# Attention and two expert layers on one core: the value product on 64x64 tiles, with whole in-weight loads

## The chip, the cores and the metric

The kernel runs on one core of a Trainium2 chip. The core has a matrix engine (TensorE; PE is its matmuls, PEld its loads of weights), a vector engine (DVE), a scalar engine (ACT), GpSimd (POOL) and a sync engine (SP), which here issues every DMA. The metric is device time in microseconds. Three runs of the kernel before gave 1185.9, 1187.23 and 1188.79 us; the median is 1187.23 us.

## The reference

```python
def _attn_ref(q, k, v, mem_k, mem_v):          # (4, 8, 768, 64); memory: 8 tokens a head
    chunk, left_ctx, right_ctx = (32, 16, 8)
    for c in range(nc):
        ...
        k_full = np.concatenate([mem_k, k_ctx], axis=2)
        v_full = np.concatenate([mem_v, v_ctx], axis=2)
        scores = scale * np.matmul(q_c, k_full.transpose(0, 1, 3, 2))
        scores = scores - np.max(scores, axis=-1, keepdims=True)
        a = np.exp(scores)
        a = a / (np.sum(a, axis=-1, keepdims=True) + 1e-09)
        out[:, :, c_start:c_end] = np.matmul(a, v_full)

def _moe_ref(x, w_in, w_out):                  # 3072 tokens, 512 -> 2048 -> 512
    h = x @ w_in
    g = h * (1.0 / (1.0 + np.exp(-1.702 * h)))
    return (g @ w_out).astype(np.float32)

def _moe2_ref(x, w_gate, w_val, w_out):        # 512 -> 1536 -> 512
    g = x @ w_gate
    silu = g * (1.0 / (1.0 + np.exp(-g)))
    val = x @ w_val
    return (silu * val @ w_out).astype(np.float32)
```

Attention runs in chunks of 32 queries, each over 64 keys (8 memory tokens, 16 to the left, 32, 8 to the right). Its output, with the heads side by side as 512 features, goes through the two feed-forward layers.

## The kernel before

The 3072 tokens are 24 groups of 128 tokens (four chunks of 32) and six blocks of four groups. For each group the kernel computes the scores of 8 heads, the exponents and their sums on DVE and ACT, and weights divided by the sums. The matrix engine turns the weights (`turn`, L153), so that the keys lie along the partitions: partition 64e + k holds key k of head 2a + e, with a from 0 to 3. `keep_e` copies them from PSUM to `ebd` (L162). The value product (`values`, L169) takes from there. `keep_x` and, in the first block, `hi_x` and `lo_x` copy the result to where the first layer reads it, and `store_x` writes it to memory.

Before the change `ebd` is block diagonal: for a pair a and a chunk c it holds 64 columns, 32 for each head e, and zeros in the other head's 64 rows, which two memsets (`zero`, L674) write once. A matmul of the value product therefore has all 128 rows, the 64 features of two heads' values as stationary columns (`v[:, a + j, c, :]`) and 64 moving columns. The result of pair a + j goes to partitions 64j and up, so that features stand in the order (pair within two, head). To match, the first layer's in-weights are loaded with their rows in that order: `load_raw` splits each of these tiles into two DMAs with a rearranged source (L276), for the 16 pairs of tiles that hold in-weights. All other weight tiles come in one DMA (L271).

The work of the opening is written out as a list of short names (`OPENING`), which sets the order of every engine: `ldq`, `ldk`, `ldv`, `ldw` are loads (queries, keys, values, weights), `sc` scores, `te` the turn, `ec` the copies of `keep_e`, `pv` the value product, `ua` and `ub` the first products with the in-weights (L542), `z` memsets. In the opening the scores of the first eight groups use 64-row tiles (L706), with the two heads' scores in two PSUM banks; later groups use a block-diagonal key tile and 128 rows (L196). After the opening the attention of blocks 2 to 5 is laid between the products of the first layer (L446 up, L581 down) at fixed places of a unit. SP's order after the opening is left to the scheduler.

Of the kernel before, what the change touches and what calls it, by code (L numbers as in the profile page):

```python
# [10 lines left out]
F32 = mybir.dt.float32  # L11
# [8 lines left out]
P = 128  # L20
B, H, S, D = 4, 8, 768, 64
NM = 8
CH, LEFT, RIGHT = 32, 16, 8
# [7 lines left out]
HP = H // 2  # L31
KC = DM // P
NF1, NF2 = FF1 // P, FF2 // P
BLK = 512
NBLK = NT // BLK
GRP = BLK // P
# [21 lines left out]
def tile_attention_moe_moe(  # L58
# [8 lines left out]
    nc = tc.nc  # L67
# [24 lines left out]
    def bank(name):  # L92
        return psum["p"].tile([P, BLK], F32, tag="p", name=name)
# [3 lines left out]
    apool = attn_ctx.enter_context(tc.tile_pool(name="attn", bufs=1))  # L97
    kbd = apool.tile([P, 2, HP, 4, KW], F32, name="kbd")
    vm = [apool.tile([P, HP, 4, D], F32, name=f"vm{i}") for i in range(2)]
    ebd = [apool.tile([P, HP, 4, 2, CH], F32, name="ebd")]  # L100

    qt, et, rt, xq, xf = {}, {}, {}, {}, {}

    def off_diagonal(t, eng):
        eng.memset(t[0:64, 1], 0.0)
        eng.memset(t[64:128, 0], 0.0)
# [43 lines left out]
    def turn(ps, t):  # L150
        ps = ps.rearrange("p (a q) -> p a q", a=HP)
        for a in range(HP):
            nc.tensor.transpose(ps[:, a, :], t[:, 2 * a : 2 * a + 2, :], ident)  # L153
        return ps

    def weights_at(g):
        return ebd[g % 2 if g < 2 * GRP else 0]

    def keep_e(g, ps, engs):
        for e, copy in enumerate(engs):  # L160
            r = slice(64 * e, 64 * e + 64)
            copy(weights_at(g)[r, :, :, e, :], ps[r].rearrange("p a (c q) -> p a c q", c=4))  # L162

    def values(g, ps, v):
        ps = ps.rearrange("p (a q) -> p a q", a=KC)
        for a in range(0, HP, 2):
            for c in range(4):
                for j in range(2):
                    nc.tensor.matmul(  # L169
                        ps[64 * j : 64 * j + 64, a : a + 2, CH * c : CH * c + CH],  # L170
                        v[:, a + j, c, :],
                        weights_at(g)[:, a + j, c].rearrange("p e q -> p (e q)"),
                        start=True,
                        stop=True,
                    )
        return ps

    def keep_x(g, ps):
# [27 lines left out]
        st_exp(g)  # L206

    def st_et(g):
        keep_e(g, turn(bank("ps_t"), et.pop(g)), (nc.scalar.copy,) * 2)

    def st_pv(g):
        ps = values(g, bank("ps_o"), vm[g % 2])
        if g + 2 < NG:
            load_kv("v", g + 2)
        keep_x(g, ps)
        store_x(g)
# [42 lines left out]
    raws = []  # L259
    AT = (0, 1, 4, 5, 2, 3, 6, 7)  # L260

    def load_raw(upto):
        while len(raws) < min(upto, NRAW):
            i = len(raws)
            if RB <= i < RB + len(spare_raw):
                raws.append(spare_raw[i - RB])
            else:
                raws.append(rpool.tile([P, 512], I64, tag="raw", name="raw", bufs=RB))
            k = AT[i] if i < len(AT) else i
            if k >= 2 * NF1 or k % 4 > 1:  # L270
                nc.sync.dma_start(out=raws[-1], in_=wr[k])  # L271
                continue
            src = wr[k].rearrange("(e d) (b a n) -> a d b e n", e=2, b=2, a=2)
            for a in range(2):
                dst = raws[-1][64 * a : 64 * a + 64].rearrange("d (b e n) -> d b e n", b=2, e=2)
                nc.sync.dma_start(out=dst, in_=src[a])  # L276

    nraw, bits = [2 * len(AT)], {}

# [21 lines left out]
    def next_weights(out):  # L301

        i = nraw[0]
        load_raw(i + RB)
        nraw[0] += 1
        take_words(i)
        yield 0
        shift_words(i)
        yield 0
        join_words(i)  # L310
        out += [bits.pop(i), raws[i]]
# [338 lines left out]
    spare = [wt["spare", i].rearrange("p s n -> p (s n)") for i in range(SPARE)]  # L650
# [1 line left out]
    k_open = [kbd[:, g] for g in range(2)]  # L652
    k_open += [spare[6 + i].bitcast(F32).rearrange("p (a c k) -> p a c k", a=HP, c=4) for i in range(6)]
    v_open = vm + [spare[12].bitcast(F32).rearrange("p (a c d) -> p a c d", a=HP, c=4)]
    ebd.append(spare[13].bitcast(F32).rearrange("p (a c e q) -> p a c e q", a=HP, c=4, e=2))
    for i in range(SPARE):
        give_w(("spare", i))
    xh, xl = [[bpool.tile([P, 2, BLK], F32R, tag="b", name=n) for _ in range(2)] for n in ("xh", "xl")]
    V, G = nc.vector, nc.gpsimd
    firsts, pairs, at, tok = [[None] * 2 for _ in range(PLAIN)], [], {}, []  # L660
# [7 lines left out]
            qt[g] = pairs[-1][:, g % 2].bitcast(F32).rearrange("p (a q) -> p a q", a=HP)  # L668
        nc.sync.dma_start(out=qt[g], in_=qg[g])

    def zero(n):
        if n < 2:
            for e in range(2):
                (V, G)[n].memset(ebd[n][64 * e : 64 * e + 64, :, :, 1 - e, :], 0.0)  # L674
        else:
            off_diagonal(kbd, G)

    def table():
        t = apool.tile([P, H], F32, tag="m", name="t", bufs=2)
# [69 lines left out]
    def values_first(g):  # L749
        at["x", g] = values(g, bank("ps_v"), vm[g % 2] if g >= 2 * GRP else v_open[g % 3])  # L750
# [118 lines left out]
    def tokens():  # L869
# [3 lines left out]

    DO = {
        "z": zero,
        "tb": lambda _: table(),
        "ldq": load_q,
        "ldk": lambda g: load_kv_first("k", g),
        "ldv": lambda g: load_kv_first("v", g),
        "ldw": lambda i: load_raw(i + 1),  # L880
        "st": store_x,
        "sc": scores_first,
# [4 lines left out]
        "rc": st_reciprocal,  # L887
        "wg": weigh_first,
        "te": turned,
        "ec": lambda g: keep_e(g, at.pop(("e", g)), (nc.scalar.copy,) * 2),  # L890
        "pv": values_first,
        "hi": hi_x,
        "xf": keep_first,
# [55 lines left out]
        "ts": lambda k, *e: tokens().sum(k, *e),  # L949
    }  # L950
    OPENING = """
        z0 tb0 z1 ldq0 ldk0 ldw0 ldq1 ldk1 ldk2 ldk3 ldq2 sc0 ldq3 mx0 pr0 ldw1 cs0 ex0 ldq4 ct0 sc1 ldv0 sm0
        wa0 wal0 ra0 ldv1 mx1 z2 ldq5 sc2 ldk4 rc0 ex1 wg0 ldk5 sm1 te0 mx2 ra1 sc3 ec0 ldw2 rc1 wg1 ex2 ldk6
        pr1 sm2 ldk7 te1 cs1 ra2 rc2 ct1 ldq6 pv0 ec1 wg2 ldq7 sumA0 mx3 wb0 ldv2 wv0 te2 hi0 wvl0 sc4 ex3 ldv3
        wbl0 xl0 ec2 sumB0 sm3 sc5 mx4 ra3 xf0 pv1 ldw3 hiB0 rc3 ex4 loB0 wg3 ldv4 pr2 mx5 te3 hi1 ldw4 ec3 cs2
# [47 lines left out]
    def attention(b):  # L1003
        gs = range(GRP * b, GRP * b + GRP)
        steps = [[(st_scores, gs[0])]]
        for g in gs:
            steps.append([(st_et, g)] + ([(st_scores, g + 1)] if g < gs[-1] else []))
            steps.append([(st_pv, g)])
        return steps
# [25 lines left out]
    for n, (ph, b, ua, ub) in enumerate(seq):  # L1035
# [6 lines left out]
        for u in range(ua, ub):  # L1042
# [47 lines left out]
            if u == ua and nxt is not None and not attends:  # L1090
                src = {1: xd, 2: yd}[nxt[0]][nxt[1]]
# [55 lines left out]
```

## Time and profile before

| | PE busy | DVE | ACT | POOL |
|---|---|---|---|---|
| whole span, 1184.9 us | 1151.1 (97%) | 653.3 (55%) | 568.2 (48%) | 342.4 (29%) |
| 0 to 19.3 us | 7.09 | 9.46 | 6.29 | 4.80 |
| 19.3 to 40.4 us | 13.62 | 16.19 | 14.17 | 7.48 |
| 140 to 278 us | 137.34 | 82.63 | 70.99 | 21.16 |

The profiled execution's span, from its first to its last instruction, is 1184.9 us; the runs' times are 1185.9 us and up, and what lies between is outside the span. Times of the table are busy us in each stretch. A busy engine is one with an instruction in flight; matmuls overlap one another, so 97% does not say that the array is full. A matmul in f32 leaves two records in the trace, each with its load of weights.

### The profile page before, as it was taken

Reading aid. Unit: us, or ns where it says so; the run is one execution under the profiler, and the core shown is the slowest. Engines: PE = TensorE matmul, PEld = TensorE weight load, DVE = VectorE, ACT = ScalarE, POOL = GpSimd, SP = SyncE. Lnnn points to the kernel's source line nnn. Section 1 sums busy time; section 2 is a strip of 40 time slices with the busy share of each in tenths; the row PEclk is TensorE's granted clock in tenths of the full one; section 3 lists DMA queues with packets and bytes.
Section 4 is the critical chain, followed back from the end, with each engine's and each line's share of the span. In section 5 each row is a group of like instructions: output and inputs, shape, how many; then the busy total and the mean of one; then the engine's idle time right before and its main releaser. Section 6 shows DMA issues by size and latency. Waiting matters only on the chain.

```text
span 1184.9 us, 22299 instructions
## 1 busy us (share of the span) xinstructions
PE 1151.1 (97%) x8908; PEld 1038.1 (88%) x8908; DVE 653.3 (55%) x1129; ACT 568.2 (48%) x1185; POOL 342.4 (29%) x309
## 2 busy tenths in 40 slices
PE   4899999999999999999999999999999999999998
PEld 3778788888899999999998989999999999999997
DVE  6786756565765444443456555354565554454553
ACT  5776554545565454444455544343445533243342
POOL 3354230203544242321235433021345521021110
PEclk9899999999999999999999999999999999999999
DMA  9986644351452322421333321210225130320302
GB/s 319 286 260 188 169 134 140 111 160 60 137 170 98 117 80 90 142 69 57 107 119 113 108 90 36 72 71 1 90 90 177 36 106 2 108 98 11 108 25 83
DMA packets 62920, 131.47 MB, mean 111 GB/s; under 512 B 5728, under 2 KB 26208, under 8 KB 60512
## 3 DMA queue, kind: packets, MB, share of 16 engines
q1 hardware_dynamic: 62816, 130.05, 35.0%
q8 instruction: 70, 1.15, 0.4%
q14 instruction: 34, 0.28, 0.1%
HBM read 98.57 MB, written 31.46 MB: 110 GB/s over the span
## 4 chain that ended last, share of the span: by engine, by line
PE 87%; DMA 4%; DVE 4%; ACT 2%; issue 2%; SPq 0%; POOL 0%; DVEq 0%; ACTq 0%; POOLq 0%
PE y L581 36%; PE ps_a L446 27%; PE ps_c L446 12%; PE ps_b L446 8%; PE ps_s L196 1%; PE ps_o L169 1%; DMA vm<-in_vg 1%; DMA w<-in_kg 1%; PE ps_u L542 1%; DMA qq<-in_qg 1%; DMA xd<-xf 1%; PE ps_t L153 1%; DMA raw<-in_wr 1%; PE ps_v L169 1%; DVE b L432 0%
## 5 line engine op out<-in xcount | busy, mean ns | idle before, releaser
L446 PEld LDWEIGHTS ps_a<-b,w 128*128 128x128 f32 x2832 | 384.0, 189 | 40.1 <-DVE ps_a L498 6.1
L446 PE MATMUL ps_a<-b,w 128*128 128x256 f32 x2832 | 397.6, 283 | 5.5 <-DVE ps_a L498 3.5
L581 PE MATMUL y<-gs,w 128*128 128x512 f32 x1152 | 298.2, 394 | 0.9 <-DVE e L742 0.5
L581 PE MATMUL y<-w,gs 128*128 128x512 f32 x864 | 247.9, 395 | 0.6 <-DVE gs L561 0.4
L581 PEld LDWEIGHTS y<-gs,w 128*128 128x128 f32 x1152 | 204.2, 189 | 36.8 <-DVE gs L561 1.2
L446 PE MATMUL ps_c<-b,w 128*128 128x256 f32 x1224 | 179.1, 282 | 0.0
L446 PEld LDWEIGHTS ps_c<-b,w 128*128 128x128 f32 x1224 | 167.1, 190 | 8.8
L581 PEld LDWEIGHTS y<-w,gs 128*128 128x128 f32 x864 | 144.1, 190 | 14.7 <-DVE gs L561 2.1
L253 POOL TENSOR_TENSOR w<-wf,w 128x512 fp32r<-128x512 f32 (+1 forms) x66 | 76.3, 1158 | 232.2 <-ACT w L250 214.8
L446 PE MATMUL ps_b<-b,w 128*128 128x256 f32 x900 | 133.7, 285 | 1.1 <-ACT m L847 0.8
L446 PEld LDWEIGHTS ps_b<-b,w 128*128 128x128 f32 x900 | 118.9, 191 | 4.6 <-issue 1.5
L549 ACT ACTIVATE g<-ps_b 128x512 f32<-128x512 f32 x72 | 43.1, 598 | 166.6 <-DVE ps_b L504 166.6
L432 DVE TENSOR_TENSOR b<-xl,b 128x512 fp32r<-128x512 f32 x72 | 64.7, 898 | 80.4 <-ACT b L428 80.2
L498 DVE TENSOR_TENSOR ps_a<-m,ps_a 128x256 f32<-128x256 f32 x115 | 49.0, 426 | 105.4 <-PE ps_a L446 99.3
L488 ACT COPY u<-ps_a 128x256 f32<-128x256 f32 x115 | 43.0, 374 | 106.6 <-PE ps_a L446 106.4
L411 POOL TENSOR_TENSOR xl<-xl,t 128x512 f32<-128x512 f32 x18 | 23.3, 1295 | 231.2 <-DVE t L408 229.9
L561 DVE TENSOR_TENSOR gs<-ps_a,gs 128x512 fp32r<-128x512 f32 x118 | 80.9, 685 | 10.2 <-ACT gs L557 9.9
L483 DVE TENSOR_TENSOR ps_b<-p,ps_b 128x256 f32<-128x256 f32 x115 | 49.2, 428 | 61.0 <-PE ps_b L446 54.8
L557 ACT CAST gs<-ps_a 128x512 fp32r<-128x512 f32 x118 | 69.8, 592 | 23.0 <-DVE ps_a L527 15.8
L527 DVE TENSOR_TENSOR ps_a<-g,ps_a 128x512 f32<-128x512 f32 x72 | 50.0, 694 | 45.7 <-PE ps_a L446 45.2
L479 ACT COPY p<-ps_a 128x256 f32<-128x256 f32 x115 | 43.0, 374 | 59.9 <-PE ps_a L446 55.9
L504 DVE TENSOR_TENSOR ps_b<-u,ps_c 128x256 f32<-128x256 f32 x102 | 43.5, 427 | 50.1 <-PE ps_c L446 49.8
(131 smaller groups left out, 1181.4 us busy)
## 6 DMA issues: line engine op xcount, KB each, us to landing
raw<-in_wr SPq DMA_DIRECT2D x49, 512.0 KB, 3.4
xl<-yd SPq DMA_DIRECT2D x12, 1024.0 KB, 4.8
vm<-in_vg SPq DMA_DIRECT2D x22, 512.0 KB, 4.6
kbd<-in_kg SPq DMA_DIRECT2D x32, 256.0 KB, 4.2
raw<-in_wr SPq DMA_DIRECT2D x30, 256.0 KB, 5.0
yp<-o SPq DMA_DIRECT2D x24, 256.0 KB, 2.7
xl<-xd SPq DMA_DIRECT2D x6, 1024.0 KB, 4.8
base<-yp SPq DMA_DIRECT2D x24, 256.0 KB, 3.4
```

The source lines that it names most:

```text
L253: eng.tensor_sub(w[:, 1, o : o + n], f, w[:, 0, o : o + n].bitcast(F32))
L432: (eng or self.engs[k]).tensor_sub(x[:, 1], self.source(k), x[:, 0].bitcast(F32))
L446: nc.tensor.matmul(ps, w[:, a, o + kc * P : o + kc * P + P], x[:, c, kc, :], start=(start and kc == 0 and (a, c) == PASSES[0]), stop=(kc = ...
L479: nc.scalar.copy(p1, ca[:, :n])
L483: add(cb[:, :n], p1, cb[:, :n])
L498: add(ca[:, n:], m, ca[:, :n])
L504: add(cb[:, n:], u2, cc)
L527: late[0] = [lambda: nc.vector.tensor_mul(ca, t, ca), lambda: gs.append(cast(ca))]
L549: nc.scalar.activation(t, c, AF.Silu)
L557: nc.scalar.copy(x[:, 0], g)
L561: nc.vector.tensor_sub(x[:, 1], g, x[:, 0].bitcast(F32))
L581: nc.tensor.matmul(y, lhs, rhs, start=(first and o == 0 and (a, c) == PASSES[0]), stop=(ends and o == len(gs) - 1 and (a, c) == passes[-1]),)
```

## The change

The value product is computed head by head: 64 rows (the keys of one head), 64 stationary columns (its features) and 32 moving columns (the queries of one chunk), into partitions 64e and up. `ebd` and its zeros go; the turned weights are copied once, as they stand, into `ek`, which has two buffers. The features then stand in their natural order, and the in-weight tiles are loaded whole, in one DMA each.

```diff
-    ebd = [apool.tile([P, HP, 4, 2, CH], F32, name="ebd")]
+    ek = [apool.tile([P, HP, P], F32, name=f"ek{i}") for i in range(2)]
...
-    def keep_e(g, ps, engs):
-        for e, copy in enumerate(engs):
-            r = slice(64 * e, 64 * e + 64)
-            copy(weights_at(g)[r, :, :, e, :], ps[r].rearrange("p a (c q) -> p a c q", c=4))
+    def keep_e(g, ps):
+        nc.scalar.copy(ek[g % 2], ps)
 
     def values(g, ps, v):
         ps = ps.rearrange("p (a q) -> p a q", a=KC)
-        for a in range(0, HP, 2):
+        for a in range(HP):
             for c in range(4):
-                for j in range(2):
-                    nc.tensor.matmul(
-                        ps[64 * j : 64 * j + 64, a : a + 2, CH * c : CH * c + CH],
-                        v[:, a + j, c, :],
-                        weights_at(g)[:, a + j, c].rearrange("p e q -> p (e q)"),
-                        start=True,
-                        stop=True,
-                    )
+                q = slice(CH * c, CH * c + CH)
+                for e in range(2):
+                    h = slice(64 * e, 64 * e + 64)
+                    nc.tensor.matmul(ps[h, a, q], v[h, a, c, :], ek[g % 2][h, a, q], start=True, stop=True)
...
-            k = AT[i] if i < len(AT) else i
-            if k >= 2 * NF1 or k % 4 > 1:
-                nc.sync.dma_start(out=raws[-1], in_=wr[k])
-                continue
-            src = wr[k].rearrange("(e d) (b a n) -> a d b e n", e=2, b=2, a=2)
-            for a in range(2):
-                dst = raws[-1][64 * a : 64 * a + 64].rearrange("d (b e n) -> d b e n", b=2, e=2)
-                nc.sync.dma_start(out=dst, in_=src[a])
+            nc.sync.dma_start(out=raws[-1], in_=wr[AT[i] if i < len(AT) else i])
...
-    def zero(n):
-        if n < 2:
-            for e in range(2):
-                (V, G)[n].memset(ebd[n][64 * e : 64 * e + 64, :, :, 1 - e, :], 0.0)
-        else:
-            off_diagonal(kbd, G)
+    def zero(_):
+        off_diagonal(kbd, G)
...
-        z0 tb0 z1 ldq0 ldk0 ldw0 ldq1 ldk1 ldk2 ldk3 ldq2 sc0 ldq3 mx0 pr0 ldw1 cs0 ex0 ldq4 ct0 sc1 ldv0 sm0
+        tb0 ldq0 ldk0 ldw0 ldq1 ldk1 ldk2 ldk3 ldq2 sc0 ldq3 mx0 pr0 ldw1 cs0 ex0 ldq4 ct0 sc1 ldv0 sm0
```

The order of PE around the third and fourth value bursts of the opening, before (`ps_v` is the result, `ps_t` the turned weights, `ps_k` scores, `ps_u` the first products with the in-weights):

```order
L706 MATMUL ps_k_128<-w,qq 32x64 x32
L169 MATMUL ps_v<-ebd,w 64x2x32 x16
L169 MATMUL ps_v<-w,vm_117 64x2x32 x16
L706 MATMUL ps_k_128<-w,qq 32x64 x32
L153 MATMUL ps_t<-ident,e 128x128 x4
L542 MATMUL ps_u<-xh,w 128x512 x8
```

Each of the two bursts is 16 matmuls of 64 moving columns (2x32). The same place of PE's order after the change:

```order
L685 MATMUL ps_k_129<-w,qq 32x64 x32
L166 MATMUL ps_v<-ek_119,w 64x32 x32
L166 MATMUL ps_v<-ek_120,vm_117 64x32 x32
L685 MATMUL ps_k_129<-w,qq 32x64 x32
L153 MATMUL ps_t<-ident,e 128x128 x4
L526 MATMUL ps_u<-xh,w 128x512 x8
```

Nothing else stands in another place on PE: each value burst has 32 matmuls with 32 moving columns in place of 16 with 64.

The start of SP's order of issues, before (`q`, `qq` queries, `kbd` and `w` from `in_kg` keys, `raw` and `w` from `in_wr` weights, `vm` and `w` from `in_vg` values):

```order
L276 DMA raw<-in_wr 64x4x128 x2
L669 DMA q<-in_qg 128x512
L689 DMA vm_117<-in_vg 128x1024
L689 DMA vm_118<-in_vg 128x1024
L669 DMA q<-in_qg 128x512
L687 DMA w<-in_kg 128x1024 x2
L276 DMA raw<-in_wr 64x4x128 x2
L687 DMA w<-in_kg 128x1024 x2
L669 DMA qq<-in_qg 128x512 x2
L689 DMA w<-in_vg 128x1024
L689 DMA vm_117<-in_vg 128x1024
L276 DMA w<-in_wr 64x4x128 x2
```

Each in-weight tile is two issues here (x2). The same place of SP's order after the change:

```order
L260 DMA raw<-in_wr 128x512
L652 DMA q<-in_qg 128x512
L668 DMA vm_117<-in_vg 128x1024
L668 DMA vm_118<-in_vg 128x1024
L652 DMA q<-in_qg 128x512
L666 DMA w<-in_kg 128x1024 x2
L260 DMA raw<-in_wr 128x512
L666 DMA w<-in_kg 128x1024 x2
L652 DMA qq<-in_qg 128x512 x2
L668 DMA w<-in_vg 128x1024
L668 DMA vm_117<-in_vg 128x1024
L260 DMA w<-in_wr 128x512
```

Each in-weight tile takes one issue in place of two, at the same place; one more such tile is issued ahead of these rows. The first `vm_117` row is the values of the first group, the second one those of the fourth.

## Rows read from the trace of the kernel before

**Rows 1.** The page's span and its busy times

```profile
span 1184.9 us, 22299 instructions
...
PE 1151.1 (97%) x8908; PEld 1038.1 (88%) x8908; DVE 653.3 (55%) x1129; ACT 568.2 (48%) x1185; POOL 342.4 (29%) x309
```

**Rows 2.** Stretches: us, busy us of PE, PEld, DVE, ACT, POOL; PEclk, DMA share, GB/s

```profile
19.30:40.40 21.10, 13.62 (x397) 11.40 (x397) 16.19 (x34) 14.17 (x33) 7.48 (x10) 0.83 1.05 330
40.40:95.00 54.60, 51.60 (x578) 42.17 (x577) 44.33 (x76) 41.37 (x82) 24.60 (x22) 0.97 0.88 264
95.00:140.00 45.00, 42.26 (x315) 36.71 (x315) 32.95 (x54) 25.36 (x52) 18.27 (x14) 1.00 0.53 153
140.00:278.00 138.00, 137.34 (x1396) 118.48 (x1395) 82.63 (x145) 70.99 (x147) 21.16 (x17) 1.00 0.47 133
```

**Rows 3.** The chain of waits, opening: start us, us, what

```profile
24.52 10.62 DMA vm<-in_vg
...
35.28 1.72 PE ps_v L169 x32
...
37.25 1.84 issue
...
40.79 6.79 PE ps_u L542 x24
...
48.69 0.58 ACT ebd L162
```

**Rows 4.** Timeline around the first value burst after 140 us

```profile
141.14 0.81 PEld L446 LDWEIGHTS ps_a<-b,w 128*128 128x128 f32 x6
141.28 0.88 PE L446 MATMUL ps_a<-b,w 128*128 128x256 f32 x6
...
142.09 1.15 PE L169 MATMUL ps_o<-ebd,vm 128*64 128x64 f32 x32
...
143.17 0.98 PE L446 MATMUL ps_b<-b,w 128*128 128x256 f32 x6
```

**Rows 5.** Instructions of `ps_o` in that burst: ns min/median/max

```profile
L169 PE MATMUL ps_o<-ebd,vm x32: 222/222/270, 142.1 to 143.0; 128*64 128x64 f32 x32
```

**Rows 6.** The same of `ps_k`, one group's scores on 64 rows

```profile
L706 PE MATMUL ps_k<-w,q x64: 213/216/240, 24.5 to 25.1; 64*32 64x64 f32 x64
```

**Rows 7.** The same of `ps_s`, one group's scores on 128 rows

```profile
L196 PE MATMUL ps_s<-kbd,q x32: 272/273/297, 57.4 to 58.3; 128*32 128x128 f32 x32
```

**Rows 8.** The same of `ps_o`, whole trace (twelve bursts)

```profile
L169 PE MATMUL ps_o<-ebd,vm x384: 222/222/270, 142.1 to 277.3; 128*64 128x64 f32 x192
L183 ACT COPY xf<-ps_o x12: 587/589/590, 143.3 to 277.5; 128x512 f32<-128x512 f32 x12
```

**Rows 9.** Whom PE waited for, 40 to 140 us

```profile
PE ps_a L446 <- DVE ps_a L498: 1.5, 1, 1.5
PE ps_s L196 <- ACT w L250: 1.1, 1, 1.1
```

**Rows 10.** Instructions of line 162, the copies of the weights

```profile
L162 ACT COPY ebd<-ps_t x40: 566/580/587, 16.1 to 275.0; 64x512 f32<-64x512 f32 x40
```

**Rows 11.** Timeline of the first 20 us

```profile
0.91 1.11 DVE L674 MEMSET ebd<- 64x512 f32 x2 [0.91 <-PEq L1136]
...
5.04 1.17 PE L706 MATMUL ps_k<-kbd,q 64*32 64x64 f32 x64 [5.04 <-DMA kbd<-in_kg]
```

**Rows 12.** The same columns for short stretches of the opening

```profile
4.50:6.50 2.00, 1.17 (x64) 0.96 (x64) 0.26 (x1) 0.00 (x0) 0.00 (x0) 1.00 1.04 254
9.00:12.00 3.00, 1.17 (x64) 0.96 (x64) 1.08 (x4) 0.62 (x1) 2.00 (x2) 1.00 1.02 401
...
16.00:19.00 3.00, 2.20 (x69) 1.76 (x68) 1.49 (x3) 1.74 (x3) 0.00 (x0) 1.00 1.04 405
```

**Rows 13.** Timeline, 18 to 64 us

```profile
24.50 0.86 PE L706 MATMUL ps_k<-w,q 64*32 64x64 f32 x64 [0.29 <-DMA w<-in_kg]
...
32.86 1.98 PE L169 MATMUL ps_v<-ebd,w 128*64 128x64 f32 x32 [0.36 <-DMA w<-in_vg]
```

More of the change, by code (lines that the diff above doesn't have):

```diff
@@ L154, in turn @@
         return ps
-    def weights_at(g):
-        return ebd[g % 2 if g < 2 * GRP else 0]
-    def keep_e(g, ps, engs):
-        for e, copy in enumerate(engs):
-            r = slice(64 * e, 64 * e + 64)
-            copy(weights_at(g)[r, :, :, e, :], ps[r].rearrange("p a (c q) -> p a c q", c=4))
+    def keep_e(g, ps):
+        nc.scalar.copy(ek[g % 2], ps)
     def values(g, ps, v):
         ps = ps.rearrange("p (a q) -> p a q", a=KC)
-        for a in range(0, HP, 2):
+        for a in range(HP):
             for c in range(4):
-                for j in range(2):
-                    nc.tensor.matmul(
-                        ps[64 * j : 64 * j + 64, a : a + 2, CH * c : CH * c + CH],
-                        v[:, a + j, c, :],
-                        weights_at(g)[:, a + j, c].rearrange("p e q -> p (e q)"),
-                        start=True,
-                        stop=True,
-                    )
+                q = slice(CH * c, CH * c + CH)
+                for e in range(2):
+                    h = slice(64 * e, 64 * e + 64)
+                    nc.tensor.matmul(ps[h, a, q], v[h, a, c, :], ek[g % 2][h, a, q], start=True, stop=True)
         return ps
@@ L208, in st_et @@
     def st_et(g):
-        keep_e(g, turn(bank("ps_t"), et.pop(g)), (nc.scalar.copy,) * 2)
+        keep_e(g, turn(bank("ps_t"), et.pop(g)))
     def st_pv(g):
@@ L654, in tile_attention_moe_moe @@
     v_open = vm + [spare[12].bitcast(F32).rearrange("p (a c d) -> p a c d", a=HP, c=4)]
-    ebd.append(spare[13].bitcast(F32).rearrange("p (a c e q) -> p a c e q", a=HP, c=4, e=2))
     for i in range(SPARE):
@@ L889, in tile_attention_moe_moe @@
         "te": turned,
-        "ec": lambda g: keep_e(g, at.pop(("e", g)), (nc.scalar.copy,) * 2),
+        "ec": lambda g: keep_e(g, at.pop(("e", g))),
         "pv": values_first,
```

## The prediction

> **What bounds the kernel now.** I read the busy line first: PE is busy for 97% of the 1184.9 us [rows 1]. The stretches split that up [rows 2]. From 140 to 278 us PE is busy 137.34 of 138 us, so any time added to PE there is added to the end. From 40.4 to 95 us it is idle 3.0 us, from 95 to 140 us 2.7 us. From 19.3 to 40.4 us it is idle 7.5 us, and there the DMA share is 1.05: the loads set the pace. The chain of waits says the same [rows 3]: a load of the values, issued at 24.52, lands after 10.62 us, then come one value burst, the scores of a group, a 1.84 us stretch in which PE waits for nothing the profile shows, and at 40.79 the first in-weight products. From there PE has little idle time. So the change has two prices: what it does to PE after 40 us, and what it does to the loads before.
>
> **The value product.** The kernel computes it in 24 bursts, one for each group of 128 tokens. One burst is now 16 matmuls, which the trace shows as 32 loads of weights and 32 matmuls of 64 moving columns (an f32 matmul leaves two records of each), and takes 1.15 us, of which the last 0.222 us is the end of the last matmul [rows 4, 5]. The other 0.93 us are 16 rounds of 0.058 us, in each of which the two column halves (j = 0 and 1) work side by side. After the change a burst is 32 matmuls, 64 records, each with 64 stationary columns as before, but 32 moving ones. Again two of them can work side by side (e = 0 and 1, on opposite corners of the array), so there are 32 rounds. What does a round cost?
>
> The trace has no such matmul, so I bound it. From below by the moving columns alone: half of 64, so half of 0.058, 0.029 us, a burst of the same length; it can't get shorter, since 64 times 32 columns are as many as 32 times 64. From above by a load of weights that hides behind nothing. The first matmul of a burst shows how long that is, because it waits for its own load: it takes 270 ns against 222 ns for the others with 64 stationary columns [rows 5], 240 against 216 with 32 columns on 64 rows [rows 6], 297 against 273 with 32 columns on 128 rows [rows 7]. So a load costs 24 ns for each 32 columns whatever the rows, and 48 ns for the 64 columns here. Without any overlap a round is 0.048 + 0.029 and some ns of turning round, about 0.085 us.
>
> I take the middle: the load of the next weights runs beside the matmul of the present ones, but does not get further ahead than one. The six loads and six matmuls of a product that starts at 141.14 are busy 0.81 and 0.88 us within the same 1.0 us [rows 4], so loads do run beneath matmuls. But a tile can then not go faster than its loads: 48 ns and the turning round, for which the present round of 0.058 us is the nearest row (there 64 stationary and 64 moving columns are matched). Halving the moving columns then saves nothing, and 32 rounds of 0.058 us are 1.86 us: **+0.93 us for each burst**. The Trainium skill (TensorE: Matmul & The Clock Gate, Part 3, "The mechanism") says that a load overlaps matmuls in flight only when its row group differs, which would make a round about 0.085 us here and the whole sum some 15 us more. The trace speaks against it, since the six loads just named use all 128 rows, as their matmuls do; I keep it as a rival below.
>
> Twelve bursts lie between 140 and 278 us [rows 8], where PE has no slack [rows 2]: 12 x 0.93 = **+11.2 us**. Eight lie between 50 and 95 us: 8 x 0.93 = 7.4 us. There PE waits now and then for others, 5.7 us in all up to 140 us; the longest wait, 1.5 us, is for a DVE addition [rows 9]. A wait for an engine that works on regardless becomes shorter when PE comes later. I let a quarter of this idle time vanish: **+5.9 us**, with 1.7 us (all idle time absorbed) and 7.4 us as the ends.
>
> **The copies of the weights.** Two ACT copies of 64 partitions, 0.58 us each [rows 10], become one of 128 partitions; the copy of the value result has that shape and takes 0.59 us [rows 8]. ACT is relieved of 24 x 0.58 = 14 us, but it is busy 71 of 138 us in the stretch with twelve of them [rows 2], and the value bursts there follow without a gap. Before 95 us a copy stands on the chain itself (48.69) [rows 3]. I take **-1 us**, between 0 and twelve bursts' -7. The weights also get two buffers for all groups rather than one after the eighth; no burst waits for that now. The two memsets that go (about 1.1 us of DVE and POOL) are over before the first scores start at 5.04, which wait for a load [rows 11]: nothing.
>
> **The loads.** The in-weight tile now comes as two DMAs whose contiguous runs in memory are 1 KB (128 words of 8 bytes), and will come as one with runs of 4 KB. In the DMA-bound opening this shows as rate: 254 GB/s in a stretch of such loads against 401 and 405 GB/s in stretches of loads with longer runs, all with the DMA engines fully busy [rows 12]. A tile of 0.524 MB is 2.1 us at 254 and 1.3 us at 405, so each load saves 0.8 us of all sixteen engines. The Trainium skill (DMA: Bandwidth & Descriptors, Specifications) gives 512 B as the least transfer for full rate; by that the gain would be nothing. The measured rates differ at full busy share, so I go by them. Three such loads are issued ahead of the values that land at 35.15 (the issue order of SP shows it): -2.5 us for that landing. The later ones fall into stretches that PE bounds.
>
> Against this stand the first four bursts. The first two have idle PE time behind them. The third and the fourth ran at a lower clock (1.98 and 1.72 us, the clock of that stretch is 0.83 on the mean [rows 2, 3, 13]) and stand right before the scores on the chain; they grow by 0.93 us each at full clock, up to 1.9 us each at half. What follows is a stall of PE of 1.84 us [rows 3], in which part of this can disappear. Together 0 to +3.7 us, and I take +2.0. The opening is thus 2.0 - 2.5 = **-0.5 us**, between -2.5 and +1.2.
>
> **The sum.** 11.2 + 5.9 - 1 - 0.5 = +15.6 us on the span of 1184.9 us, 1200.5 us. The median of the runs is 1187.2 us, 2.3 us above that span; with the same 2.3 us the forecast is **1203 us**. All the lower ends together give 11.2 + 1.7 - 7 - 2.5 = +3.4 us, 1191 us; all the upper ones 11.2 + 7.4 - 0 + 1.2 = +19.8 us, 1207 us; a round longer by 0.005 us would add 0.16 us to each of 20 bursts, another 3 us. Its own range is 1191 to 1210 us.
>
> **Rivals.**
> *The loads of weights do not pace the burst (faster).* If a tile can hold more than one set of weights ahead, rounds are 0.029 us and PE gains no work. Then only the opening and the copies count: -2.5 - 1 = -3.5 us, 1184 us. It decides as soon as a round costs less than 0.033 us, where 20 bursts add under 3 us. For it: scores with 64 rows and 32 stationary columns run 64 records in 0.86 us [rows 13], so many small tiles do work side by side. Against it: there the stationary columns are half as many as the moving ones, here twice, and the 48 ns that a load of 64 columns takes are longer than the 29 ns of its matmul, so the loads could keep up only if two of one tile ran at once, which no row shows. Chance 0.12.
> *Loads and matmuls of a tile, or the two corners of the array, take turns.* Rounds of 0.085 us make a burst 2.72 us, +1.79 us; 20 of them less 3.5 us are +32 us, 1219 us. The sentence of the Trainium skill above is one reason; another is that both corners write into one PSUM bank, which the Trainium skill (TensorEngine Tiling (Array Packing), Gotcha 1) does not allow for different row tiles at once. In this kernel's compact scores the two row halves go to two banks, so no row shows them in one. Against it: the two column halves of now share a bank too, and the overlap named above. Chance 0.07.
> *The early bursts are absorbed.* If the eight bursts before 95 us cost only 1.7 us and the opening gains its full 2.5 us, the sum is 11.2 + 1.7 - 1 - 2.5 = +9.4 us, 1197 us, inside the range of the forecast. For it: DVE and ACT, which PE waits for there, are not held up by the change. Against it: PE is busy 94% of that time, and a wait vanishes only if its cause does not itself come from PE. Chance 0.10.
>
> **How the numbers follow.** The forecast has 0.71, the rivals 0.12, 0.07 and 0.10. A difference of 0.2% (2.4 us) is about what a measurement of this kernel can tell from none. Faster: most of the first rival, 0.10. The same: the rest of it, with rounds a little above 0.029 us, 0.03. Slower: 0.87. The range 1191 to 1210 us holds the forecast and the third rival, and leaves out the other two, which have 0.19.
>
> **What the changed profile would show.** A value burst in the 140 to 278 us stretch takes 2.0 to 2.1 us from the first start to the last end where the step on the loads of weights is right, 1.1 to 1.2 us where it is wrong, and over 2.7 us where they take turns. That stretch as a whole grows by 11 us with PE busy throughout. ACT has 24 copies of 0.59 us from the transposed weights. The values that land at 35.15 us now land two to three us earlier, while the first in-weight products start within 2 us of 40.4 us. In-weight tiles show some 400 GB/s. Everything after 278 us keeps its length. The forecast fails if the bursts stay at 1.15 us, or if the early ones make no difference to the start of the stretch at 140 us.

## The result and the profile after

The changed kernel takes **1204.6 us** (median of 4 runs, 1203.3 to 1205.3), the kernel before, run beside it, 1187.1 us. The ratio is 1.0144, with a 95% interval of 1.0129 to 1.0158: it is slower by 17.5 us, and the forecast was 1203. The page after, its span and busy lines and the row of the queue that brings the program itself, answers to [rows 1]:

```profile
span 1202.5 us, 23777 instructions
...
PE 1175.1 (98%) x9676; PEld 1064.5 (89%) x9676; DVE 652.0 (54%) x1127; ACT 552.1 (46%) x1161; POOL 340.8 (28%) x307
...
q8 instruction: 76, 1.25, 0.4%
```

The span is 17.6 us longer, and PE is busy 24.0 us more: 768 more matmul records on PE and as many loads of weights on PEld. ACT is relieved of 16 us, and nothing that can be measured came of it (the run with two copies, below). The stretches, with the columns of [rows 2]:

```profile
19.30:40.40 21.10, 18.87 (x449) 17.54 (x447) 13.25 (x28) 9.76 (x24) 6.72 (x8) 1.00 0.83 310
40.40:95.00 54.60, 52.37 (x753) 44.21 (x752) 43.52 (x75) 35.49 (x73) 24.34 (x23) 1.00 0.77 233
95.00:140.00 45.00, 42.58 (x396) 37.64 (x395) 31.03 (x49) 23.70 (x50) 19.25 (x15) 1.00 0.46 150
140.00:278.00 138.00, 137.21 (x1610) 119.78 (x1608) 80.74 (x141) 60.26 (x128) 21.13 (x17) 1.00 0.48 136
...
30.00:33.00 3.00, 3.00 (x80) 2.60 (x79) 0.95 (x3) 1.17 (x4) 0.00 (x0) 1.00 0.20 36
```

The first row has turned over. Between 19.3 and 40.4 us PE was idle for 7.5 us and the DMA engines were full; now PE is idle for 2.2 us and the DMA share is 0.83. From 30 to 33 us the DMA engines stand nearly still while PE works without a pause: the loads wait for PE there, not PE for the loads. The value instructions of the twelve late bursts, and the copies of the weights (ns min/median/max, first and last start), answer to [rows 5, 8, 10]:

```profile
L166 PEld LDWEIGHTS ps_o<-ek,vm x768: 129/135/135, 148.7 to 294.8; 64*64 64x64 f32 x192
L166 PE MATMUL ps_o<-ek,vm x768: 219/219/240, 148.7 to 294.8; 64*64 64x32 f32 x192
...
L157 ACT COPY ek<-ps_t x24: 567/585/592, 15.7 to 291.0; 128x512 f32<-128x512 f32 x24
```

The moving columns are halved, and the matmul takes 219 ns where it took 222. The timeline of PE shows the opening value bursts, one after 50 us, and the first of the late ones:

```profile
18.60 3.63 PE L166 MATMUL ps_v<-ek,vm 64*64 64x32 f32 x64
...
25.18 1.06 PE L166 MATMUL ps_v<-ek,vm 64*64 64x32 f32 x15
28.47 2.87 PE L166 MATMUL ps_v<-ek,vm 64*64 64x32 f32 x49 [2.23 <-issue]
...
33.43 3.62 PE L166 MATMUL ps_v<-ek,w 64*64 64x32 f32 x64
36.86 3.60 PE L166 MATMUL ps_v<-ek,vm 64*64 64x32 f32 x64
...
52.01 2.06 PE L166 MATMUL ps_v<-ek,vm 64*64 64x32 f32 x64
...
148.70 2.06 PE L166 MATMUL ps_o<-ek,vm 64*64 64x32 f32 x64
150.68 0.98 PE L430 MATMUL ps_b<-b,w 128*128 128x256 f32 x6
```

A burst is 2.06 us where it was 1.15 [rows 4]. The first late burst starts 6.6 us later than before (148.70 against 142.09) and the last record of the last one 17.5 us (294.8 against 277.3): 10.9 us grow between them, and nothing behind them. The four opening bursts take 3.6 us each (the second is split by a stall). The same instructions that take 219 ns from 52 us on take 291 there, and the transposes and scores beside them are slow too. These lengths are those of the lower of the two levels of TensorE's clock. The clock column prints 1.00 for this stretch only because this trace has no record of the clock before 44 us. The trace of the run with two copies (below) has one: its third and fourth burst take the same 3.62 and 3.60 us, and there the column says 0.50:

```profile
30.00:40.00 10.00, 10.00 (x215) 9.44 (x213) 5.46 (x12) 5.35 (x13) 1.27 (x1) 0.50 0.78 283
```

The chain of waits, with the columns of [rows 3]:

```profile
18.67 3.56 PE ps_v L166 x64
22.23 1.04 PE ps_t L153 x4
23.27 1.98 PE ps_k L685 x125
25.25 0.99 PE ps_v L166 x15
26.24 2.23 issue
28.47 2.87 PE ps_v L166 x49
31.34 1.04 PE ps_t L153 x4
32.38 1.12 PE ps_k L685 x63
33.50 6.97 PE ps_v L166 x128
40.47 1.11 PE ps_k L685 x61
41.58 1.04 PE ps_t L153 x4
42.62 2.40 PE ps_u L526 x7
```

Before, a load of the values stood on the chain for 10.6 us. Now PE stands on it without a break from 18.67 us on, but for one stall of 2.23 us, and the first in-weight products start at 42.62 instead of 40.79 us.

### The profile page after: what moved, and what is told of

The parts are those of the page before. It is cut to its first block, busy times and chain, and to the rows that moved or that the text cites. A ratio compares the mean times of both kernels' runs of the same rounds, so it can differ in the third digit from the quotient of the medians.

```text
span 1202.5 us, 23777 instructions
## 1 busy us (share of the span) xinstructions
PE 1175.1 (98%) x9676; PEld 1064.5 (89%) x9676; DVE 652.0 (54%) x1127; ACT 552.1 (46%) x1161; POOL 340.8 (28%) x307
## 4 chain that ended last, share of the span: by engine, by line
PE 90%; DVE 4%; issue 2%; ACT 2%; DMA 1%; POOL 1%; SPq 0%; DVEq 0%; ACTq 0%; POOLq 0%
PE y L565 35%; PE ps_a L430 27%; PE ps_c L430 12%; PE ps_b L430 8%; PE ps_v L166 2%; PE ps_o L166 2%; PE ps_s L187 1%; PE ps_t L153 1%; PE ps_u L526 1%; DMA kbd<-in_kg 1%; PE ps_k L685 1%; DVE b L416 0%; ACT b L412 0%; DVE t L392 0%; DVE gs L545 0%
## 5 line engine op out<-in xcount | busy, mean ns | idle before, releaser
L541 ACT CAST gs<-ps_a 128x512 fp32r<-128x512 f32 x118 | 69.8, 591 | 23.4 <-DVE ps_a L511 15.8
L463 ACT COPY p<-ps_a 128x256 f32<-128x256 f32 x115 | 43.0, 373 | 59.7 <-PE ps_a L430 55.7
```

What stands on the lines that cost most here:

```text
L463: nc.scalar.copy(p1, ca[:, :n])
L541: nc.scalar.copy(x[:, 0], g)
```

## The experiments

The kernel before took 1187.7 to 1187.8 us beside each of these runs. The changed kernel once more, unedited, to compare with the others:

> The changed kernel itself, beside the three others on one chip: 1.014 times the kernel before, about 1204.5 us, by every theory.

Measured: 1203.6 us (1203.2 to 1204.1), ratio 1.0133 (1.0119 to 1.0146). The edits of the changed kernel below are set against this second measurement, which lies 1.0 us under the first.

**Do the loads of weights pace the burst?** The moving operand is doubled to 64 columns where the row allows it (three of four chunks), with the same instructions and stationary columns.

```diff
-                q = slice(CH * c, CH * c + CH)
+                q = slice(CH * c, min(CH * c + 2 * CH, P))
```

> The changed kernel, but chunks 0 to 2 of each pair multiply 64 moving columns (the chunk's own 32 and the next chunk's, which the next matmul writes over), the last chunk 32 as before. Theory (loads of weights pace a round): 64 stationary columns stay, so a round stays at 0.058 us, a burst between 140 and 290 us at 2.05 us, and the whole within 2 us of the changed kernel's 1204.6 us. Rival (load and matmul of a tile take turns, so that 0.058 us is 0.029 + 0.029): 24 of 32 rounds grow by 0.027 us, a burst becomes about 2.7 us, and the whole 1204.6 + 20 x 0.65 = about 1217 us.

Measured: 1201.75 us (1200.9 to 1203.7), ratio 1.012 (1.0102 to 1.0138). Its first late burst, on PE's timeline:

```profile
146.67 2.06 PE L166 MATMUL ps_o<-ek,vm 64*64 64x64 f32 x64
```

With twice the moving columns the burst has the same 2.06 us. So the moving columns do not pace it. The time as a whole is 2.9 us under the 1204.6 us of the expectation, not within 2 us; against the second measurement it is 1.9 us, and there the intervals overlap. In the traces the difference lies in the opening, where the clock rose earlier and the third and fourth burst take 2.55 and 2.03 us instead of 3.6.

The other side of the test: the stationary columns of each matmul are split into two halves of 32, so that a burst has twice as many matmuls.

```diff
-                    nc.tensor.matmul(ps[h, a, q], v[h, a, c, :], ek[g % 2][h, a, q], start=True, stop=True)
+                    for f in range(2):
+                        o = 64 * e + 32 * f
+                        nc.tensor.matmul(ps[o : o + 32, a, q], v[h, a, c, 32 * f : 32 * f + 32], ek[g % 2][h, a, q], ...)
```

> The changed kernel, but each head's 64 features are taken as two halves of 32 stationary columns, on 64x32 tiles: 64 matmuls a burst (128 records), four tiles side by side. Theory (loads of weights pace a round): a load of 32 columns takes half, a round of four about 0.029 us, 32 rounds; a burst of 1.1 to 1.3 us, so nearly all of the 18 us that the bursts cost come back: 1186 to 1190 us. If the whole loads are worth their 2.5 us in the opening too, 1183 to 1186 us. Rival (the number of matmuls paces: 0.029 us for each record, as in the changed kernel): a burst of 3.9 us, 1204.6 + 20 x 1.85 = about 1240 us.

Measured: 1212.3 us (1209.5 to 1214.0), ratio 1.0204 (1.0186 to 1.0222). PE's timeline, a piece of the opening and the first late burst:

```profile
36.91 0.34 PE L168 MATMUL ps_v<-ek,vm 64*32 64x32 f32 x8
41.67 1.77 PE L168 MATMUL ps_v<-ek,vm 64*32 64x32 f32 x116 [4.42 <-issue]
...
46.65 1.10 PE L689 MATMUL ps_k<-w,qq 64*32 64x64 f32 x56 [2.96 <-issue]
...
164.59 1.29 PE L168 MATMUL ps_o<-ek,vm 64*32 64x32 f32 x128
```

Half the stationary columns bring the burst from 2.06 to 1.29 us although it has twice the instructions: the loads pace it. But the time went up, not down, and that expectation fell. From the first late burst to the end of the last, 139.7 us pass instead of 146.3; that is 6.6 of the 9.2 us by which twelve bursts are shorter, and two stalls of 1.0 and 1.5 us took the rest. The part ahead of them lost 15.9 us (the first late burst starts at 164.59 instead of 148.70), mostly in stalls in which PE waits for nothing that the profile shows. Up to 110 us they sum to 21.8 us (15.9 in seven before `ps_v`, 5.9 in two before `ps_k`; the kernel before has 3.0 in three, the changed kernel 2.2 in one). The clock was at its lower level for much of this part too: the column says 0.50 from 30 to 50 us. The page counts 26849 instructions and 88 packets on the instruction queue, against 23777 and 76 of the changed kernel and 22299 and 70 before: one packet more for every 250 instructions or so. In the longest of these stalls (37.2 to 41.7 us) that queue moves one packet, while the loads keep the DMA engines busy at 94%; around the changed kernel's stall (25.5 to 28.5 us) it moves one at 93%.

**Is it the number of instructions?** The kernel before, its value product split in the same way: 64 records as in the changed kernel, and no longer burst.

```diff
-                    nc.tensor.matmul(
-                        ps[64 * j : 64 * j + 64, a : a + 2, CH * c : CH * c + CH], v[:, a + j, c, :], ...)
+                    for f in range(2):
+                        o = 64 * j + 32 * f
+                        nc.tensor.matmul(
+                            ps[o : o + 32, a : a + 2, CH * c : CH * c + CH], v[:, a + j, c, 32 * f : 32 * f + 32], ...)
```

> The kernel before with each 64 stationary columns of the value product taken as two of 32, on 128x32 tiles: as many matmuls as in the changed kernel (64 records a burst) with the rows and moving columns of before, so that a burst stays at 1.1 to 1.3 us and the result the same. It measures the number of instructions alone. Theory (PE's stalls in the opening are its wait for instructions, which queue behind the loads): PE stalls 2 to 6 us more before 95 us, and the whole is 1190 to 1194 us; after 140 us nothing changes. Rival (instructions cost nothing, the stalls have another cause): within 1.5 us of the kernel before.

Measured: 1192.1 us (1190.2 to 1192.7), ratio 1.0032 (1.002 to 1.0044), +4.3 us. PE's timeline:

```profile
34.10 0.53 PE L171 MATMUL ps_v<-ebd,w 128*32 128x64 f32 x9
38.22 1.61 PE L171 MATMUL ps_v<-ebd,w 128*32 128x64 f32 x52 [3.59 <-issue]
...
148.51 1.10 PE L171 MATMUL ps_o<-ebd,vm 128*32 128x64 f32 x64
```

The late burst is no longer than before (1.10 against 1.15 us), yet the kernel loses 4.3 us. Its stalls without a shown cause are 9.4 us up to 110 us, against 3.0, and it has about as many instructions (23837) and as many instruction packets (76) as the changed kernel. Twice the value instructions in a DMA-bound opening thus cost time though the burst is no longer. The count alone does not set the stalls: the changed kernel, with as many, has 2.2 us of them. That the fetch of the program is what PE waits for fits the counts and the places, but it was not tried apart. A rival is the clock: in this trace the transposes take 1.11 us until 46 us, as at the lower level, which the kernel before had left for a while by 23 us. The next run answers it.

**What are the twelve late bursts worth?** The kernel before, with 64x64 tiles from the 13th group on.

```diff
+        if g >= 3 * GRP:
+            for a in range(HP):
+                for c in range(4):
+                    for e in range(2):
+                        h = slice(64 * e, 64 * e + 64)
+                        nc.tensor.matmul(ps[h, a, CH * c : CH * c + CH], v[h, a, c, :], weights_at(g)[h, a, c, e], ...)
+            return ps
```

> The kernel before, with the changed kernel's 64x64 tiles for the last twelve groups alone (those between 140 and 280 us), read from the diagonal of the block-diagonal weights; the features of these groups then stand in another order than the in-weights, which changes the result and not the work. Theory: 12 bursts of 2.05 instead of 1.15 us with no slack on PE: +10.9 us, 1198 to 1199 us. So the other 9 us of the value product lie in the first twelve groups. Rival (waits after 140 us absorb part of it): +7 us or less.

Measured: 1198.65 us (1197.5 to 1199.0), ratio 1.0089 (1.0075 to 1.0103): +10.9 us, which is 12 x 0.905 (0.905 us is what a burst grows by).

Up to the 13th group this kernel is the kernel before, and in its trace, too, the transposes take 1.11 us until 43 us, and the four opening bursts 1.97 to 1.98 us. PE's last scores and its first in-weight products, in this run and then in the one above:

```profile
41.11 1.10 PE L715 MATMUL ps_k<-w,qq 64*32 64x64 f32 x56 [0.91 <-issue]
...
42.91 2.68 PE L551 MATMUL ps_u<-xh,w 128*128 128x512 f32 x8
```

```profile
44.38 1.10 PE L708 MATMUL ps_k<-w,qq 64*32 64x64 f32 x56 [2.38 <-issue]
...
46.19 3.76 PE L544 MATMUL ps_u<-xh,w 128*128 128x512 f32 x8
```

With the clock low in both until then, the run with more instructions comes to these products 3.3 us later, with 9.4 us of such stalls against 0.9. So the clock does not explain the delay, by these two traces. And the opening of before, which starts them at 40.44 us in one trace and at 42.91 in another, shows how far single traces of one opening can lie apart.

**What are the whole loads worth?** The value product and copies of before, whole in-weight loads; the heads are paired in another order in the inputs as they are laid out, which makes the rows of a whole tile come out right.

```diff
-            k = AT[i] if i < len(AT) else i
-            if k >= 2 * NF1 or k % 4 > 1:
...
+            nc.sync.dma_start(out=raws[-1], in_=wr[AT[i] if i < len(AT) else i])
...
-    q, k, v, mk, mv = (x[n] for n in ("q", "k", "v", "mem_k", "mem_v"))
+    heads = [2 * (p - p % 2 + e) + p % 2 for p in range(HP) for e in range(2)]
+    q, k, v, mk, mv = (x[n][:, heads] for n in ("q", "k", "v", "mem_k", "mem_v"))
```

> The kernel before with its value product, its block-diagonal weights and their two copies, but with heads paired in another order in the laid out inputs, so that the features come out in their natural order and the in-weight tiles are loaded whole. Theory (the loads bound the opening): 0.8 us less for each of three loads ahead of the values that let the first in-weight products start, so these start 2 to 3 us before 40.4 us and the whole is 1184 to 1185 us. Rival (the opening is bound by PE at its lower clock and by DVE, and the loads are hidden): within 1 us of the kernel before, 1187 us.

Measured: **1181.3 us** (1180.4 to 1181.8), ratio 0.9944 (0.9933 to 0.9956): faster than both kernels, by 6.5 us than before, and below the 1184 to 1185 us of the expectation. The stretch that was DMA-bound, to be set against the first of [rows 2]:

```profile
19.30:40.40 21.10, 15.14 (x413) 12.99 (x410) 17.58 (x38) 17.19 (x40) 10.32 (x13) 0.92 1.03 400
```

At the same DMA share the loads move 400 GB/s where they moved 330, PE does more by 40.4 us, and the in-weight products start at 36.6 instead of 40.4 us. (The edit makes the runs in memory longer and also makes one DMA of two; which of them counts was not tried apart.)

The reverse: the changed kernel with the two DMAs of before for each in-weight tile.

```diff
-            nc.sync.dma_start(out=raws[-1], in_=wr[AT[i] if i < len(AT) else i])
+            k = AT[i] if i < len(AT) else i
+            if k >= 2 * NF1 or k % 4 > 1:
+                nc.sync.dma_start(out=raws[-1], in_=wr[k])
+                continue
+            ...
```

> The changed kernel with the split in-weight loads of the kernel before; the rows of the in-weights then stand in another order than the features, which changes the result and not the work. Theory (the opening of the changed kernel is bound by PE at the lower clock, not by the loads): within 1.5 us of the changed kernel, 1204.6 us. Rival (the loads bound the opening, and whole loads are worth 2.5 us there): about 1207 us or more.

Measured: 1207.7 us (1206.3 to 1208.1), ratio 1.0166 (1.0151 to 1.018): 4.1 us above the changed kernel's second measurement and 3.1 above its first. The theory of this expectation fell, and its rival's time came: even where PE is on the chain for the whole opening, slower loads cost time, though less than in the kernel before.

**Is one copy worth anything?** The changed kernel with two copies of 64 partitions.

```diff
-        nc.scalar.copy(ek[g % 2], ps)
+        for e in range(2):
+            r = slice(64 * e, 64 * e + 64)
+            nc.scalar.copy(ek[g % 2][r], ps[r])
```

> The changed kernel with the copy of the turned weights done again as two of 64 partitions, 0.58 us each. Theory (ACT has slack, the copies count only in the opening): 0 to 2 us more than the changed kernel. Rival (the one copy is worth half a us in each burst that PE bounds): about 8 us more.

Measured: 1202.8 us (1202.3 to 1203.7), ratio 1.0127 (1.0113 to 1.014). Its interval overlaps the changed kernel's: one copy is worth nothing that can be measured.

**What do the opening bursts cost?** Whole loads, and 64x64 tiles from the fifth group on; the four opening bursts stay as before.

```diff
+        if g >= GRP:
+            ...
+            return ps
```

> The kernel before with whole in-weight loads (heads paired in the other order, as in the run that took 1181.3 us), and with the value product on 64x64 tiles from the fifth group on: twenty bursts; the first four keep the product of before. The heads of its output come in another order. It splits the 17 to 18 us of the changed kernel into loads, later bursts and opening bursts. Theory: the twenty later bursts cost 12 x 0.905 = 10.9 us and 8 x 0.905 = 7.2 us less about 1.5 us of idle time that vanishes; 1181.3 + 10.9 + 5.7 = 1198 us (1197 to 1200). The four opening bursts of the changed kernel then cost the rest to its 1204 us, about 6 us, three times what the prediction took for them. Rival: the opening bursts cost the predicted 2 us and the eight bursts before 95 us cost more than their own length; then it takes about 1202 us.

Measured: 1197.3 us (1196.6 to 1199.2), ratio 1.0082 (1.0068 to 1.0095), which is the theory's time; the rival's 1202 is out. PE's timeline, its opening bursts and what follows them:

```profile
18.44 1.84 PE L178 MATMUL ps_v<-ebd,vm 128*64 128x64 f32 x32
...
23.29 1.15 PE L178 MATMUL ps_v<-w,vm 128*64 128x64 f32 x32
...
29.25 1.15 PE L178 MATMUL ps_v<-ebd,w 128*64 128x64 f32 x32
30.23 1.10 PE L178 MATMUL ps_v<-w,vm 128*64 128x64 f32 x32
...
34.58 1.11 PE L708 MATMUL ps_k<-w,qq 64*32 64x64 f32 x56 [2.62 <-issue]
...
36.38 2.05 PE L544 MATMUL ps_u<-xh,w 128*128 128x512 f32 x4
```

The opening bursts take 5.2 us in all, against 14.8 us in the changed kernel; the in-weight products start at 36.4 instead of 42.3 us. So the opening bursts on 64x64 tiles cost 5.9 us by the start of these products, and 6.3 us by the runs (1203.6 less 1197.3). The start is blurred by the clock: in the trace with the shorter bursts the first twelve products then ran partly at the lower level (the clock column says 0.50 from 35 to 40 us), and at the thirteenth the lead is 4.9 us.

## Why the prediction was right, step by step

The runs split the change as follows (medians; the spans give -6.3, +17.6 and +6.3). Whole loads, twenty bursts and opening bursts are steps between neighbouring kernels, so that they add up to the whole by construction; each one by itself is the finding.

| part | predicted us | measured us | from |
|---|---|---|---|
| whole loads | -2.5 | -6.5 | whole loads alone against before |
| twenty bursts after 45 us | +17.1 | +16.0 | whole loads with 64x64 from the 5th group, against whole loads alone |
| of these the twelve late ones | +11.2 | +10.9 | 64x64 from the 13th group against before |
| four opening bursts | +2.0 | +6.3 | changed kernel against whole loads with 64x64 from the 5th group |
| one copy for two | -1 | 0 | two copies in the changed kernel |
| sum | +15.6 | +15.8 | 1203.6 - 1187.8 |

- **The round, right.** A round was taken as 0.058 us, set by the load of 64 stationary columns. Measured are (2.06 - 0.219) / 32 = 0.057 us, and the same with 64 moving columns. With 32 stationary and 32 moving columns, four matmuls side by side, it is (1.29 - 0.193) / 32 = 0.034; with 32 stationary and 64 moving ones (1.10 - 0.219) / 16 = 0.055. So the longer side sets the round. An estimate from these two lengths, 32 and 64, is 0.75 ns for each column and some 10 ns beside. The rivals "the loads of weights do not pace" (0.029) and "take turns" (0.085) are both out. With the second one falls the reading of the Trainium skill (TensorE: Matmul & The Clock Gate, Part 3, "The mechanism") by which a load on the same rows does not overlap. Nor did the two corners, which write into one PSUM bank, take turns: by the prediction's sum a round would then be 85 ns, and it stayed at 57 with 64 moving columns too. (The prediction's "some 15 us more" for that round should be 17: 20 x 32 x 0.027.)
- **The late bursts, right:** 10.9 us for a forecast of 11.2, with PE busy throughout. Behind the last of them nothing changed: 907 us pass to the end in both kernels.
- **The eight bursts before 95 us, right in size.** In the changed kernel the time from the first in-weight products to the end of the last of these bursts grew by 5.3 us (42.3 to 102.0 against 40.4 to 94.8). Counted from the thirteenth of these products, where the clock is high in both, it grew by 5.9 us (56.0 against 50.2), as was taken; the other traces have 55.3 to 55.7 with 64x64 tiles and 49.9 with those of before. So some 1 to 2 us of the 7.2 (8 x 0.905) vanished, about the quarter of the idle time. All twenty bursts, with the opening bursts of before on both sides, cost 16.0 us by medians and 17.6 by spans, of which 1.7 lie ahead of the thirteenth product, where only one of the two traces has the clock low; 15.9 lie behind it, 2.2 less than 20 x 0.905. The 1.5 us wait for the DVE addition [rows 9] is still there:

```profile
PE ps_a L430 <- DVE ps_a L482: 1.5, 1, 1.5
```

- **The copies, sized a little too well:** 0 for -1, within its bounds.
- **The opening, wrong in both terms, and they cancelled.** It was taken as 2.0 - 2.5 = -0.5 us. By the runs it came out as 6.3 - 6.5 = -0.2 us, but that is luck: both terms were too small, by about 4 us each, and had one of them alone been off, the forecast would have missed by those 4 us. In the profiled pair the in-weight products start 1.8 us later, outside the bounds of -2.5 to +1.2; that number is no firmer than the 2.5 us by which two traces of the opening of before differ. The term of the loads counted only the three tiles ahead of one landing, 0.8 us each; the whole stretch from 19 to 40 us is DMA-bound, and the faster loads were worth 3.8 us by its end and 6.5 in all. The term of the bursts let the first two hide behind idle PE time and allowed at most 3.7 us for the other two. But all four ran at the lower clock, at 3.6 us, together 9.5 us more than the bursts of before take beside the same loads; 3.6 us of this (4 x 0.905) is the change at full clock, most of the rest is the clock. Of the 9.5 us some 6 stayed after the idle time was used up. So PE replaced the loads as what stands on the chain of the opening, though not wholly: loads split in two again still cost the changed kernel 3 to 4 us. The values of the fourth burst did land earlier, by 5.9 us rather than two or three: they were issued at 22.27 us, and the row of that DMA says

```profile
DMA to landing us min/median/max: 7.0/7.0/7.0
```

which is 29.3 us instead of 35.15. But PE came to them only at 36.86. The next value load was then issued at 31.37 us, where it is issued at 24.48 beside the shorter bursts.

## What to carry to other kernels

Where many small f32 matmuls run on tiles, each with its own stationary operand, count the longer of stationary and moving columns: a product that halved the moving side and doubled the number of matmuls here went from 1.15 to 2.06 us, and zeros that fill up the moving side are cheaper than a second set of weights. Judge an instruction's cost in each stage by itself: in a DMA-bound opening, more instructions can bring stalls that no wait in the profile explains (9.4 us against 0.9 and 3.0). And an edit made of two parts should be timed in parts; here the loads were worth 6.5 us, hidden beneath a product that cost 22.

## What was not expected of the hardware

- Stalls of up to 4.4 us in which PE waits for nothing shown, most of them while the DMA engines are full. Up to 110 us they sum to 3.0 us in the kernel before (22299 instructions), 9.4 in that kernel with 32 stationary columns (23837) and 21.8 with 64x32 tiles (26849, and 6.0 us more later); but in the changed kernel, with 23777, to 2.2, and in the run with 64x64 tiles from the 13th group, with 23069, to 0.9.
- Whole in-weight tiles, with longer runs in memory and one DMA for two, bring a full DMA stretch from 330 to 400 GB/s at nearly the same busy share (1.05 and 1.03).
- In the trace of the changed kernel TensorE stayed slow through the whole opening (291 ns for each value matmul until 40 us), though PE worked there without a gap from 28.5 us on; the matmuls became fast only during the first in-weight products, which start at 42.3 us. With 64 moving columns the fourth burst was already fast (218 ns, from 36.5 us on). With the bursts of before and whole loads they were fast from 23 us on (222 ns), and the clock column says 0.50 later, from 35 to 40 us. But the opening of before stayed slow until 43 us as well, in the trace of the run with 64x64 tiles from the 13th group. Why the clock rises when it does was not settled.
